# Holding back five weight transfers, and other readers, tiles and order for the last two groups of a mixture-of-experts kernel

## The chip, the cores and the metric

The kernel runs on one core of one Trainium2 chip. The metric is the device time of one execution in microseconds (us), taken as the median of several runs. The core has TensorE (PE in the profile, with its weight loads as PEld), VectorE (DVE), ScalarE (ACT), GpSimd (POOL) and SyncE (SP). SyncE only issues transfers here. GpSimd adds in SBUF and also issues the weight transfers, from the same queue of instructions.

## The reference

An attention with a feature map feeds a mixture of experts that is weighted with a balanced routing matrix P. Cut to what matters:

```python
proj = einsum('bhsd,df->bhsf', x, w_phi); proj -= max(abs(proj), -1)
phi  = concatenate([exp(proj), exp(-proj)], -1)          # for q and k
attn = (phi(q) @ (phi(k).T @ v)) / (phi(q) @ sum(phi(k)) + 1e-06)
x    = attn.transpose(0, 2, 1, 3).reshape(4608, 512)
P    = exp(x @ w_gate - max); 8 times: rows /= sum, columns /= sum, P *= N / E
out  = zeros((4608, 512))
for e in range(8):                       # w1[e]: 512 x 1024, w2[e]: 1024 x 512
    h = maximum(x @ w1[e], 0.0)
    out += P[:, e:e + 1] * (h @ w2[e])
```

There are 8 batches, 8 heads, 576 positions and a head width of 64, all float32 at the borders of the kernel.

## The kernel before

The attention, the routing and expert 0 come first. Experts 1 to 7 then run in one loop at the end of the kernel, and the change is in that loop. The 4608 tokens are nine groups: groups 0 to 7 have 512 tokens each and group 8 gathers the last 64 tokens of every batch. The sum over the experts stays in SBUF in float32, one tile `acc[g]` for each group (4 row tiles of 128 x 512). In the order listings `acc_4271` is group 6, `acc_4272` is group 7, `acc_4273` is group 8, and `acc_76` to `acc_80` with `acc_4270` are groups 0 to 5.

**Products.** Both matrix products of an expert are done with seven block products in place of eight, as Strassen and Winograd do. `up7` makes h = relu(x w1) for a pair of groups, `down7` makes h w2 for one group. The seven products of `down7` are called X1, X2, X3, X4, Y1, Z1 and Z2. X1 to X4 add up in one PSUM bank, Z1 and Z2 in another, and Y1 has a third; after each product the bank is read, because every partial sum belongs to some block of the output. Four of the products need sums of blocks of h, which VectorE makes ahead in four `S` tiles of two halves each, eight instructions (line L1013, `S<-hT`). For group 7 of the last expert these sums lie in tiles of the ring of h itself, so they read `hT<-hT`. The weights are summed in the same way (L1013, `T<-w` and `w<-w`, 1024 columns each).

**Who reads a bank.** `read` lets VectorE do acc = acc + P * bank in two instructions (L1305) where the product's name is in `by_dve`. Otherwise `read2` lets ScalarE copy the bank, scaled with P, into a tile `V` in two instructions (L1315), and GpSimd adds that tile to acc (L1319). In the usual group X2, Z2 and X4 go to VectorE and X1, Y1, Z1 and X3 go the other way. In groups 6 and 7 of the last expert the lists differ.

**Order of the work.** `ORDER` is a list written by hand that mixes the seven products of a group with the products of `up7` of groups that come later; group g's `down7` runs while later groups' h is made, so groups 6, 7 and 8 of expert e are finished while expert e + 1 has begun. The last expert takes group 8 first, and its groups 6 and 7 are left over: `END` interleaves their products by hand, "a" for group 6 and "b" for group 7. All operations are recorded with what they read and write and with a planned duration; a list scheduler, `Plan`, gives each engine its order, and the program is issued in that order. What an engine really waits for on the chip is set by the tiles that its instructions touch. A string in the lists of reads and writes, such as "sums of h", is a name that only the planner knows.

**Weights.** `load_w` (L378) asks GpSimd's queue for two transfers per expert, w1 and w2, of 2 MB in float32 each, cast to bfloat16 on the way, into two buffers each. An expert's weights are asked for about an expert ahead.

**Stores.** After the last expert SP sends acc to HBM. For groups 6 and 7 each block of two row tiles by 256 columns goes when its last product has been read (L982), and one block is cut into two transfers: `one`.

Of the kernel before, what the change touches and what calls it, by code (L numbers as in the profile page):

```python
# [228 lines left out]
def kernel(  # L229
# [16 lines left out]
    E = moe_w_gate.shape[1]  # L246
# [27 lines left out]
    acc = [accp.tile([128, 4, DD], FP32, name=f"acc{g}", tag=f"acc{g}") for g in range(NA)]  # L274
# [12 lines left out]
    late = {}  # L287
# [7 lines left out]
    def act(el, fn, r=(), w=()):  # L295
        plan.op("ACT", el / 1200.0 + 0.09, 0.22, fn, r, w)
# [4 lines left out]
    def pool(el, fn, r=(), w=()):  # L301
        plan.op("POOL", el * 1.64e-3 + 0.17, 0.25, fn, r, w, shared=True)

    def dma(queue, nbytes, rate, fn, r=(), w=()):

        plan.op(queue, 0.8 if queue == "POOL" else 0.6, 0.0, fn, r, w, (), nbytes / rate / (125 / 100))
# [52 lines left out]
    def new(tag):  # L359
        return banks.new(int(tag[1])) if tag in ("P1", "P2") else R[tag].new()  # L360

    def grant(tag, slot, ops):

        b = Buf(R[tag])
        b.slot = slot
        for o in ops:
            o.bufs.append(b)
            b.left += 1
# [6 lines left out]
    def load_w(e, r=()):  # L375
        w1, w2 = new("w1"), new("w2")
        for w, src in ((w1, moe_w1), (w2, moe_w2)):
            dma("POOL", 2 << 20, 280, lambda w=w, src=src: nc.gpsimd.dma_start(  # L378
                out=w(), in_=src[e].rearrange("(c p) f -> p c f", p=128)),
                r, [(w, i, j) for i in range(2) for j in range(2)])  # L380
        return w1, w2
# [365 lines left out]
    def xkeys(g, dc=None):  # L747
        if g < 8:
            return [("xT", g, i) for i in range(NP)] if dc is None else [("xT", g, dc)]
        return [("xTr", b, h) for b in range(B) for h in range(2)]  # L750
# [44 lines left out]
    def akey(g):  # L795
        return ["late"] * (g >= NA) + ["P"] * (g >= 9)
# [182 lines left out]
    def store(g, ts, js=(), nt=1):  # L979
        if len(js):  # L980
            cols = slice(256 * js[0], 256 * js[-1] + 256)
            dma("SP", len(js) * nt << 17, 320, lambda: nc.sync.dma_start(  # L982
                out=out[g * S:g * S + SM].rearrange("(p j) d -> p j d", j=NJ)[:, ts:ts + nt, cols],
                in_=acc[g][:, ts:ts + nt, cols]),
                [("acc", g, ts + n, j) for j in js for n in range(nt)],
                [("out", g, ts, j) for j in js])
        elif g < 8:
            if ts % 2:
                dma("SP", 1 << 19, 320, lambda: nc.sync.dma_start(
                    out=out[g * S:g * S + SM].rearrange("(p j) d -> p j d", j=NJ)  # L990
                    [:, ts - 1:ts + 1], in_=acc[g][:, ts - 1:ts + 1, :]),
                    [("acc", g, t, j) for t in (ts - 1, ts) for j in range(2)], [("out", g, ts)])
        else:
            for i in range(2):
                b = 2 * ts + i
                rows = slice(i * 64, i * 64 + 64)
                dma("SP", 1 << 17, 320, lambda b=b, rows=rows: nc.sync.dma_start(
                    out=out[b * S + SM:(b + 1) * S], in_=acc[8][rows, ts, :]),
                    [("acc", 8, ts, j) for j in range(2)], [("out", 8, b)])
# [79 lines left out]
    def pair_sums_x(p):  # L1079

        X = [new("S") for _ in range(4)]

        def x(n):
            return lambda: X[n]().rearrange("p (k a) b -> p k (a b)", k=2)

        b11, b12, b21, b22 = pq(p, 0, 1), pq(p, 0, 0), pq(p, 1, 1), pq(p, 1, 0)
        for n, y, z, r in ((0, b12, b11, ["sums of x"]), (1, b22, x(0), [X[0]]),
                           (2, b22, b12, []), (3, b21, x(1), [X[1]])):
            sub(dve, 1024, x(n), y, z, ALU.subtract,
                xkeys(2 * p) + xkeys(2 * p + 1) + ["late"] + r,  # L1090
                [X[n]] + (["sums of x"] if n == 1 else []))
            dma("SP", 1 << 18, 250, lambda n=n: nc.sync.dma_start(out=Xd[p][n], in_=x(n)()),
                [X[n]], [("Xd", p, n)])

    def sums_x(g):

        X = [new("S") for _ in range(2)]

        def x(n):
            return lambda: X[n // 2]()[:, n % 2 * 2:n % 2 * 2 + 2]  # L1100

        b11, b12, b21, b22 = xq(g, 0, 1), xq(g, 0, 0), xq(g, 1, 1), xq(g, 1, 0)
        for n, y, z, r in ((0, b12, b11, []), (1, b22, x(0), [0]), (2, b22, b12, []),
                           (3, b21, x(1), [1])):
            sub(dve, 512, x(n), y, z, ALU.subtract,
                xkeys(g) + ["late", "sums of x"] + [(X[i // 2], i % 2) for i in r]
                + ([(X[1], "slot")] if n == 2 else []),
                [(X[n // 2], n % 2)] + ([(X[1], "slot")] if n == 0 else []))
        for i in range(2):
            dma("SP", 1 << 18, 250, lambda i=i: nc.sync.dma_start(  # L1110
                out=Xd[4][i], in_=X[i]().rearrange("p (k a) b -> p k (a b)", k=2)),
                [(X[i], n) for n in range(2)], [("Xd", 4, i)])
# [129 lines left out]
    def down7(e, g, H, B7, last=False):  # L1242
# [13 lines left out]
        late = akey(g)  # L1256
# [36 lines left out]
                    r + r2 + (["P"] if e else late) + list(more), first)  # L1293

        by_dve = ("X2", "Z2", "X4")
        if e == E - 1 and g in (6, 7):
            by_dve = (("X2", "X3", "X4", "Z1", "Z2") if g == 6 else ("X3", "X4", "Z1", "Z2"))

        def read(bank, i, j, name):

# [9 lines left out]

        def read2(bank, i, j):

            u = new("V")
            for n in range(2):
                act(390, lambda n=n: nc.scalar.activation(  # L1315
                    out=u()[:, n, :], in_=bank()[:, 256 * n:256 * n + 256], func=ACT.Copy,
                    bias=0.0, scale=P[:, 4 * g + 2 * i + n, e:e + 1]), [bank, "P"],
                    [(u, n), "order of V"])
            pool(670, lambda: nc.gpsimd.tensor_tensor(  # L1319
                out=acc[g][:, 2 * i:2 * i + 2, 256 * j:256 * j + 256],  # L1320
                in0=acc[g][:, 2 * i:2 * i + 2, 256 * j:256 * j + 256], in1=u(), op=ALU.add),
                [(u, 0), (u, 1)], [("acc", g, 2 * i + n, j) for n in range(2)])

        if e == 1 and g < 9:
            for ts in range(4):
# [35 lines left out]
        def stores(names):  # L1361
            if e < E - 1:
                return
            if g not in (6, 7):
                for ts in range(4 if len(names) == len(all_) else 0):
                    store(g, ts)
                return
            for i, j, by in ((0, 0, {"X1", "Y1"}), (0, 1, {"X2", "Z2"}), (1, 1, {"Z1", "X3"}),
                             (1, 0, {"X4"})):
                if by <= names and (i, j) not in stored:  # L1370
                    stored.add((i, j))
                    one = g == 7 and (i, j) == (0, 1)
                    for n in range(2 if one else 1):
                        store(g, 2 * i + n, (j,), 1 if one else 2)

# [10 lines left out]

    ORDER = "X1 x10 w10 x11 X2 x20 y10 x21 Z1 y11 X3 w11 x30 x31 x40 x41 w20 Y1 w21 X4 Z2".split()
    END = (
        "aX1 aX2 aY1 aZ1 aZ2 bX1 aX3 bX2 bZ1 bY1 bX3 aX4 bX4 bZ2").split()
    queue = []  # L1390

    def pop():
        if not queue:
            return None
        e, g, H, B7 = queue.pop(0)
        return down7(e, g, H, B7, (e, g) == (E - 1, 7))

    for e in range(1, E):
        w1, w2 = load_w(e, ["late"])
        if e == 1:  # L1400
            for p in range(4):
                pair_sums_x(p)
            sums_x(8)
            for p in range(4):
                seen = {}
                for key in xkeys(2 * p):
                    for d in plan.readers.get(key, []):
                        seen[id(d)] = d
                grant("X", p, seen.values())
        A7, B7 = sums_w(e, w1, w2)  # L1410
        for p in (range(5) if e < E - 1 else (4, 0, 1, 2, 3)):
            X = load_x(p)
            gs = (2 * p, 2 * p + 1) if p < 4 else (8,)
            H = [[[new("hT") for _ in range(2)] for _ in range(2)] for _ in gs]
            un = up7(A7, p, X, H, ["up0"])
            for half in range(len(gs)):
                dn = pop()
                for n in ORDER:
                    if len(n) == 3:
                        un[n[:2], int(n[2]) + 2 * half]()  # L1420
                    elif dn is not None:
                        dn(n)
            queue += [(e, g, h, B7) for g, h in zip(gs, H)]
# [34 lines left out]
```

## Time and profile before

| | before |
|---|---|
| runs | 1037.2, 1037.89, 1035.61 us |
| median | 1037.2 us |
| the profiled execution: its own time / its span | 1037.74 us / 1036.0 us |
| granted TensorE clock, mean over the span | 0.997 |
| TensorE busy | 1008.2 us, 97% of the span |
| VectorE / ScalarE / GpSimd busy | 877.0 / 706.7 / 467.4 us |
| weight transfers of `load_w` and expert 0 | 14 of 1024 KB as written, median 9.2 us to landing |
| stores of acc | 12 of 512 KB and 9 smaller ones at the end |

The profile is of one execution. "Busy" counts instructions that ran, and a busy TensorE can still run at half its clock. In the rows a line is start, duration, engine, line of the code, operation, output and inputs with their shapes, and a count; square brackets give the idle time of the engine before it and who ended that. Line numbers are those of the kernel before. A row of the chain of waits says which work, or which wait, led to the end of the run.

### The profile page before, as it was taken

To read this page: it belongs to the slowest core of one execution; us is meant where nothing else is said; L and a number is where in the kernel's file an instruction comes from. 1 tells how busy PE (TensorE), PEld (TensorE's weight loads), DVE (VectorE), ACT (ScalarE), POOL (GpSimd) and SP (SyncE) were. 2 spreads that over 40 slices of the span, in tenths; PEclk is the share of its full clock that TensorE was granted. 3 is DMA by queue.
4 is the path that set the end of the run, shared out by engine and by line. 5 is a ranking of instruction groups with operands and counts; after the bars stand their busy time and mean duration, and the time that the engine had idled before them with its cause. 6 is when DMAs were issued, how large, how long until landed. Compare 5 with 4: busy or idle time off the path is not lost.

```text
span 1036.0 us, 21792 instructions
## 1 busy us (share of the span) xinstructions
PE 1008.2 (97%) x7856; PEld 692.1 (67%) x7974; DVE 877.0 (85%) x1875; ACT 706.7 (68%) x1571; POOL 467.4 (45%) x535
## 2 busy tenths in 40 slices
PE   7899999999999999999999999999999999999997
PEld 5666666644566766676667666776667666776665
DVE  7999998987787888888888888888888788887887
ACT  7999999845688766666666665666666665656662
POOL 5776775400244444444444444444444444344443
PEclk9999999999999999999999999999999999999998
DMA  9998995095311441132311341134113411204323
GB/s 254 182 170 134 187 161 103 2 229 144 75 44 50 92 82 42 42 89 60 78 41 57 77 92 43 41 62 83 46 47 92 82 42 42 62 22 123 133 92 122
DMA packets 124700, 93.77 MB, mean 91 GB/s; under 512 B 47456, under 2 KB 116640, under 8 KB 124592
## 3 DMA queue, kind: packets, MB, share of 16 engines
q1 hardware_dynamic: 90832, 68.44, 24.2%
q0 software_dynamic: 33680, 23.90, 16.5%
q8 instruction: 62, 1.02, 0.4%
q14 instruction: 46, 0.38, 0.1%
q10 hardware_dynamic: 80, 0.03, 0.0%
HBM read 94.98 MB, written 14.16 MB: 105 GB/s over the span
## 4 chain that ended last, share of the span: by engine, by line
PE 84%; DVE 5%; issue 1%; ACT 1%; DVEq 0%; ACTq 0%
PE P L1130 39%; PE P L1164 31%; PE P L484 13%; DVE acc L1305 1%; DVE hT L1194 1%; PE P L683 1%; DVE w L1013 1%; DVE hT L1013 1%; PE P L722 0%; DVE S L1013 0%; ACT q L480 0%; DVE m L476 0%; PE P L688 0%; ACT U L1190 0%; ACT hT L776 0%
## 5 line engine op out<-in xcount | busy, mean ns | idle before, releaser
L1319 POOL TENSOR_TENSOR acc<-acc,V 128x512 f32<-128x512 f32 x249 | 320.8, 1301 | 432.9 <-ACT V L1315 429.5
L1190 ACT COPY U<-P 128x512 f32<-128x512 f32 x378 | 215.8, 588 | 145.7 <-PE P L1164 81.6
L1315 ACT ACTIVATE V<-P 128x256 f32<-128x256 f32 x498 | 217.8, 476 | 127.0 <-PE P L1130 123.4
L1194 DVE CUSTOM_DVE_ANT_0 hT<-P,U 128x512 bf16<-128x512 f32 x378 | 252.6, 687 | 44.0 <-ACT U L1190 22.7
L1130 PEld LDWEIGHTS <-S 128*128 128x128 bf16 x1984 | 194.8, 98 | 55.7 <-issue 3.2
L1305 DVE SCALAR_TENSOR_TENSOR acc<-P,acc 128x256 f32<-128x256 f32 x384 | 164.3, 477 | 65.1 <-PE P L1130 62.9
L1164 PE MATMUL P<-xT,w 128*128 128x512 bf16 x674 | 191.3, 379 | 3.6 <-DVE acc L1305 2.3
L1130 PEld LDWEIGHTS <-hT 128*128 128x128 bf16 x1544 | 151.1, 98 | 57.7 <-DVE hT L1194 0.7
L1164 PE MATMUL P<-xT,T 128*128 128x512 bf16 x550 | 158.1, 379 | 1.8
L1130 PE MATMUL P<-w,hT 128*128 128x256 bf16 x1016 | 145.3, 273 | 0.4 <-DVE hT L1194 0.3
L1130 PE MATMUL P<-T,S 128*128 128x256 bf16 x1056 | 137.8, 274 | 3.1 <-DVE acc L1305 2.7
L1164 PEld LDWEIGHTS <-w 128*128 128x128 bf16 x896 | 87.6, 98 | 62.0 <-issue 0.7
L1130 PE MATMUL P<-w,S 128*128 128x256 bf16 x928 | 123.9, 274 | 0.6
L1013 DVE TENSOR_TENSOR S<-hT 128x512 bf16<-128x512 bf16 x248 | 103.1, 433 | 19.2 <-PE P L1130 18.4
L1164 PEld LDWEIGHTS <-T 128*128 128x128 bf16 x672 | 65.7, 98 | 58.9 <-issue 4.2
L476 DVE TENSOR_REDUCE m<-P 128x4 f32<-128x512 f32 x128 | 83.6, 678 | 4.0 <-PE P L484 3.1
L609 POOL TENSOR_TENSOR v<-v_m,em 128x512 bf16<-128x512 f32 x64 | 67.0, 1047 | 42.8 <-ACT em L480 38.7
L1199 ACT ACTIVATE hT<-P 128x512 bf16<-128x512 f32 x126 | 74.5, 598 | 9.9 <-PE P L1164 9.6
L484 PE MATMUL P<-xT,w 128*128 128x512 bf16 x271 | 71.7, 379 | 0.9 <-ACT q L480 0.3
L484 PE MATMUL P<-w,hT 128*128 128x512 bf16 x272 | 69.7, 379 | 0.8 <-DVE m L476 0.2
L1130 PE MATMUL P<-T,hT 128*128 128x256 bf16 x528 | 70.4, 273 | 0.1
L480 ACT ACTIVATE q<-P 128x512 bf16<-128x512 f32 x128 | 69.4, 637 | 1.2 <-PE P L484 0.9
(107 smaller groups left out, 1168.8 us busy)
## 6 DMA issues: line engine op xcount, KB each, us to landing
xT<-xd SPq DMA_DIRECT2D x168, 128.0 KB, 2.2
w<-in_moe_w_dram POOLq DMA_DIRECT2D x14, 1024.0 KB, 9.2
v_m<-in_v_dram SPq DMA_DIRECT2D x14, 512.0 KB, 4.7
out_dram<-acc SPq DMA_DIRECT2D x12, 512.0 KB, 3.1
X<-xd SPq DMA_DIRECT2D x42, 128.0 KB, 2.2
early<-xd SPq DMA_DIRECT2D x42, 128.0 KB, 2.1
xd<-S SPq DMA_DIRECT2D x18, 256.0 KB, 2.9
qk<-in_k_dram POOLq DMA_DIRECT2D x12, 256.0 KB, 5.8
```

The costliest lines, as they stand in the source:

```text
L476: dve(el, lambda: nc.vector.tensor_reduce(out=dst(), in_=src(), axis=AX.X, op=ALU.max, apply_absolute_value=True), r, w)
L480: act(el, lambda: nc.scalar.activation(out=dst(), in_=src(), func=ACT.Exp, bias=0.0, scale=scale), r, w)
L484: nc.tensor.matmul(out_, lhsT=lhsT, rhs=rhs, start=start, stop=stop)
L1013: lambda: f.tensor_tensor(out=out_(), in0=x(), in1=y(), op=op), r, w, **kw)
L1130: pe(256, lambda i=i, k=k, z=z: nc.tensor.matmul(bank()[:, 256 * i:256 * i + 256], lhsT=lhs(k, i), rhs=rhs(k), start=first and z, stop=k = ...
L1164: pe(512, lambda k=k: nc.tensor.matmul(bank[fp](), lhsT=f()[:, k, 128 * fp:128 * fp + 128], rhs=rhs(k), start=first and k == 0, stop=k == ...
L1190: act(512, lambda: nc.scalar.copy(out=u[fp][n]().rearrange("p a b -> p (a b)"), in_=x[fp]()), [x[fp]], [u[fp][n]])
L1194: dve(500, lambda: nc.vector._custom_dve(ADD_SAT, out=out_(fp, i, j), in0=halves_(bank[fp]()), in1=flat(u[fp][n]()), s0=3.0e38, s1=0.0), [ ...
L1199: act(512, lambda: nc.scalar.activation(out=out_(fp, i, j), in_=halves_(x[fp]()), func=ACT.Relu, bias=0.0, scale=1.0), [x[fp]], [okey(fp, ...
L1305: dve(330, lambda n=n, ts=ts: nc.vector.scalar_tensor_tensor(out=acc[g][:, ts, 256 * j:256 * j + 256], in0=bank()[:, 256 * n:256 * n + 256 ...
L1315: act(390, lambda n=n: nc.scalar.activation(out=u()[:, n, :], in_=bank()[:, 256 * n:256 * n + 256], func=ACT.Copy, bias=0.0, scale=P[:, 4 ...
L1319: pool(670, lambda: nc.gpsimd.tensor_tensor(out=acc[g][:, 2 * i:2 * i + 2, 256 * j:256 * j + 256], in0=acc[g][:, 2 * i:2 * i + 2, 256 * j: ...
```

## The change

Four edits. First, the weight transfers of experts 3 to 7 (those asked for while an expert above 1 is on) get a read of group 8's acc as an extra dependence, for w1 and w2. Second, the readers of banks in the last expert's groups 6 and 7 change: VectorE takes X2, X3, X4, Y1, Z1, Z2 of group 6 (before X2, X3, X4, Z1, Z2) and X2, X4, Z2 of group 7 (before X3, X4, Z1, Z2). GpSimd makes five additions in both, aX1, aY1, bX1, bX2, bY1 before and aX1, bY1, bX1, bZ1, bX3 now. Third, in these two groups ScalarE copies into `U`, a ring of four tiles, and the planner holds the additions for "sums of h". Fourth, the hand-written `END` is another one, and the block of the last stores that is cut in two is (1, 0) of group 6, whose last product is X4.

```diff
-        if e == E - 1 and g in (6, 7):
-            by_dve = (("X2", "X3", "X4", "Z1", "Z2") if g == 6 else ("X3", "X4", "Z1", "Z2"))
+        ending = e == E - 1 and g in (6, 7)
+        if ending:
+            by_dve = by_dve + ("X3", "Y1", "Z1") if g == 6 else by_dve
...
-            u = new("V")
+            u = new("U" if ending else "V")
...
-                [(u, 0), (u, 1)], [("acc", g, 2 * i + n, j) for n in range(2)])
+                [(u, 0), (u, 1)] + ["sums of h"] * ending,
+                [("acc", g, 2 * i + n, j) for n in range(2)])
...
-                    one = g == 7 and (i, j) == (0, 1)
+                    one = (g, i, j) == (6, 1, 0)
...
-        "aX1 aX2 aY1 aZ1 aZ2 bX1 aX3 bX2 bZ1 bY1 bX3 aX4 bX4 bZ2").split()
+        "aX1 bY1 aX2 bX1 bX2 bZ1 aZ1 aX3 aY1 aZ2 bX3 bX4 bZ2 aX4").split()
...
-        w1, w2 = load_w(e, ["late"])
+        w1, w2 = load_w(e, ["late"] + [("acc", 8, ts, j) for ts in range(4) for j in range(2)
+                                       if e > 1])
```

How this moves instructions is seen in two places. The first is GpSimd's queue at a weight transfer in the middle of the loop, from group 6 to the w2 transfer; the names behind `DMA` are the weight tiles, and `waits` lists the engines and transfers whose semaphores the instruction waits for. Before:

```order
L1319 TENSOR_TENSOR acc_4271<-acc_4271,V 128x2x256 [waits Activation_49] x2
L378 DMA w_8603<-in_moe_w_dram 128x4x1024 [waits DMASW6_49,DVE_49,PE_49]
L1319 TENSOR_TENSOR acc_4271<-acc_4271,V 128x2x256 [waits Activation_49,Pool_49]
L1319 TENSOR_TENSOR acc_4271<-acc_4271,V 128x2x256 [waits Activation_49]
L1319 TENSOR_TENSOR acc_4272<-acc_4272,V 128x2x256 [waits Activation_49] x2
L1319 TENSOR_TENSOR acc_4272<-acc_4272,V 128x2x256 [waits Activation_49,Pool_49]
L1319 TENSOR_TENSOR acc_4272<-acc_4272,V 128x2x256 [waits Activation_49]
L1319 TENSOR_TENSOR acc_4273<-acc_4273,V 128x2x256 [waits Activation_49] x2
L1319 TENSOR_TENSOR acc_4273<-acc_4273,V 128x2x256 [waits Activation_49,Pool_49]
L1319 TENSOR_TENSOR acc_4273<-acc_4273,V 128x2x256 [waits Activation_49]
L378 DMA w_8946<-in_moe_w_dram 128x8x512 [waits DMASW7_49,DVE_49,PE_49]
```

And now:

```order
L1320 TENSOR_TENSOR acc_4271<-acc_4271,V 128x2x256 [waits Activation_49] x2
L1320 TENSOR_TENSOR acc_4271<-acc_4271,V 128x2x256 [waits Activation_49,Pool_49]
L1320 TENSOR_TENSOR acc_4271<-acc_4271,V 128x2x256 [waits Activation_49]
L1320 TENSOR_TENSOR acc_4272<-acc_4272,V 128x2x256 [waits Activation_49] x2
L1320 TENSOR_TENSOR acc_4272<-acc_4272,V 128x2x256 [waits Activation_49,Pool_49]
L1320 TENSOR_TENSOR acc_4272<-acc_4272,V 128x2x256 [waits Activation_49]
L1320 TENSOR_TENSOR acc_4273<-acc_4273,V 128x2x256 [waits Activation_49] x2
L1320 TENSOR_TENSOR acc_4273<-acc_4273,V 128x2x256 [waits Activation_49,Pool_49]
L1320 TENSOR_TENSOR acc_4273<-acc_4273,V 128x2x256 [waits Activation_49]
L378 DMA w_8947<-in_moe_w_dram 128x4x1024 [waits DMASW6_49,DVE_49,PE_49]
L378 DMA w_8960<-in_moe_w_dram 128x8x512 [waits DMASW7_49,DVE_49,PE_49]
```

The w1 transfer has moved from the middle of group 6's four additions to behind group 8's last one, directly ahead of the w2 transfer, which stays where it was. On VectorE the sums of that tile move with it (`T<-w_8603` was the first of them, `w_8603<-w_8603` the second). Before, on VectorE, from group 8's last reads to the first reads of group 0 (`acc_76`):

```order
L1305 SCALAR_TENSOR_TENSOR acc_4273<-P,acc_4273 128x256 x4
L1013 TENSOR_TENSOR S<-hT 128x512
L1013 TENSOR_TENSOR S<-hT,S 128x512
L1013 TENSOR_TENSOR S<-S,hT 128x512
L1013 TENSOR_TENSOR T<-w_8603 128x1024
L1013 TENSOR_TENSOR S<-hT,S 128x512
L1194 ISA hT<-P,U 128x512 x2
L1013 TENSOR_TENSOR S<-hT 128x512
L1305 SCALAR_TENSOR_TENSOR acc_76<-P,acc_76 128x256 x2
```

And now, from group 0's last reads to the second sum:

```order
L1306 SCALAR_TENSOR_TENSOR acc_76<-P,acc_76 128x256 x4
L1013 TENSOR_TENSOR S<-hT,S 128x512
L1013 TENSOR_TENSOR T<-w_8947 128x1024
L1013 TENSOR_TENSOR S<-hT 128x512
L1306 SCALAR_TENSOR_TENSOR acc_77<-P,acc_77 128x256 x2
L1194 ISA hT<-P,U 128x512
L1013 TENSOR_TENSOR S<-hT 128x512
L1013 TENSOR_TENSOR w_8947<-w_8947 128x2x512
```

The first sum of w1 has moved from behind group 8's last reads to behind group 0's. The sum in place, which stood ahead of group 1's first reads (`acc_77`), follows them.

The second place is GpSimd's queue in the last two groups of the last expert. Before:

```order
L1319 TENSOR_TENSOR acc_4271<-acc_4271,V 128x2x256 [waits Activation_49]
L1319 TENSOR_TENSOR acc_4271<-acc_4271,V 128x2x256 [waits Activation_49,Pool_49]
L1319 TENSOR_TENSOR acc_4272<-acc_4272,V 128x2x256 [waits Activation_49]
L1319 TENSOR_TENSOR acc_4272<-acc_4272,V 128x2x256 [waits DVE_49,Activation_49]
L1319 TENSOR_TENSOR acc_4272<-acc_4272,V 128x2x256 [waits Activation_49,Pool_49]
```

And now:

```order
L1320 TENSOR_TENSOR acc_4271<-acc_4271,U 128x2x256 [waits Activation_49]
L1320 TENSOR_TENSOR acc_4272<-acc_4272,U 128x2x256 [waits Activation_49]
L1320 TENSOR_TENSOR acc_4272<-acc_4272,U 128x2x256 [waits Activation_49,Pool_49]
L1320 TENSOR_TENSOR acc_4272<-acc_4272,U 128x2x256 [waits Activation_49]
L1320 TENSOR_TENSOR acc_4272<-acc_4272,U 128x2x256 [waits Activation_49,Pool_49]
```

The second addition went to group 6's block of the first one and waited for it; now it goes to group 7's and waits for ScalarE alone. No addition waits for VectorE any more, and the sums of h stand on VectorE where they stood, eight in a row behind group 6's.

## The prediction

> **What bounds the kernel now.** I read the page first, then who TensorE waited for from 300 us on (the loop over the experts), then the chain of waits and the timeline of the last 25 us. The page's lines on the engines, the granted clock and the chain:
>
> ```profile
> span 1036.0 us, 21792 instructions
> ...
> PE 1008.2 (97%) x7856; PEld 692.1 (67%) x7974; DVE 877.0 (85%) x1875; ACT 706.7 (68%) x1571; POOL 467.4 (45%) x535
> PEclk9999999999999999999999999999999999999998
> PE 84%; DVE 5%; issue 1%; ACT 1%; DVEq 0%; ACTq 0%
> ```
>
> TensorE bounds it: 97% busy at full clock in all but the last slice. The change removes no product, so it can only win where TensorE stands still or is slow. The waits of TensorE between 300 and 1010 us, and the chain of waits at the end:
>
> ```profile
> PE P L1164 <- DVE acc L1305: 2.3, 4, 0.6
> ...
> 1016.18 5.90 DVE hT L1013 x8
> 1022.08 0.80 DVE acc L1305 x2
> 1022.88 0.04 issue
> 1022.92 6.48 PE P L1130 x42
> ```
>
> So there are two targets: four waits of 0.6 us at the borders of experts, and one stretch at the end where VectorE's eight sums for group 7 hold TensorE. The windows of the end show both prices of that stretch (window, length, busy PE, PEld, DVE, ACT, POOL, then granted clock):
>
> ```profile
> 1019.60:1023.03 3.43, 0.69 (x8) 0.47 (x6) 3.43 (x5) 0.84 (x2) 2.05 (x2) 1.00 0.21 76
> 1023.03:1026.44 3.41, 3.41 (x18) 2.35 (x17) 1.50 (x4) 0.00 (x0) 0.00 (x0) 0.50 0.00 0
> 1026.44:1029.80 3.36, 3.36 (x32) 2.95 (x31) 2.93 (x7) 1.57 (x4) 1.42 (x2) 1.00 0.44 156
> ```
>
> TensorE is nearly idle in the first, and in the second it runs at clock 0.50, which costs 3.41 x 0.50 = 1.7 us.
>
> **The w1 transfers.** One of the four waits, in the timeline of GpSimd, VectorE and TensorE, with a free sum of the same form as the last row:
>
> ```profile
> 570.41 0.79 POOL L378 DMA_DIRECT2D w<-in_moe_w_dram  x1 [2.19 <-PE P L1130]
> 571.23 2.50 POOL L1319 TENSOR_TENSOR acc<-acc,V 128x512 f32<-128x512 f32 x2
> 572.05 2.23 DVE L1013 TENSOR_TENSOR w<-w 128x1024 bf16<-128x1024 bf16 x1
> 574.93 0.38 PE L1164 MATMUL P<-xT,w 128*128 128x512 bf16 x1
> 575.90 0.38 PE L1164 MATMUL P<-xT,w 128*128 128x512 bf16 x1 [0.59 <-DVE acc L1305]
> 573.85 0.81 PE L1164 MATMUL P<-xT,w 128*128 128x512 bf16 x3
> 350.63 0.68 DVE L1013 TENSOR_TENSOR w<-w 128x1024 bf16<-128x1024 bf16 x1
> ```
>
> The transfer holds GpSimd's queue to 571.2, its two additions then run back to back to 573.73, and the weight sum, issued at 572.05 in the middle of the first, ends only at 574.28: 2.23 us where 0.68 is free. A sum of two SBUF tiles doesn't get in between two additions that follow each other without a gap. The reads behind it come late, and TensorE starts its next matmul 0.97 us after the last; three in 0.81 us are (0.81 - 0.38) / 2 = 0.22 apart, so 0.75 us is lost. What stands there without a transfer is seen at the last expert, for which no weights are asked any more:
>
> ```profile
> 901.89 2.50 POOL L1319 TENSOR_TENSOR acc<-acc,V 128x512 f32<-128x512 f32 x2 [2.58 <-ACT V L1315]
> 903.14 1.79 DVE L1013 TENSOR_TENSOR T<-w 128x1024 bf16<-128x1024 bf16 x1
> 906.04 0.89 PE L1130 MATMUL P<-xT,w 128*128 128x256 bf16 x4
> 905.60 0.60 PE L1130 MATMUL P<-X,T 128*128 128x256 bf16 x4
> ```
>
> The additions start 1.25 us ahead of the sum instead of 0.82, the sum takes 1.79, and four matmuls take 0.89 where four take 0.60: 0.29 lost. So the move gives 0.75 - 0.29 = 0.46 at each of four borders, -1.8 us. Bounds: nothing, if the additions wait for ScalarE anyway, and 4 x 0.75 = -3.0, if the sum escapes both additions.
>
> At its new place the transfer stands behind group 8's last addition. Who waits for it there:
>
> ```profile
> 598.54 0.92 POOL L378 DMA_DIRECT2D w<-in_moe_w_dram  x1
> 602.92 2.71 POOL L1319 TENSOR_TENSOR acc<-acc,V 128x512 f32<-128x512 f32 x2 [3.46 <-ACT V L1315]
> ...
> 613.61 0.68 DVE L1013 TENSOR_TENSOR w<-w 128x1024 bf16<-128x1024 bf16 x1
> DMA to landing us min/median/max: 8.1/9.2/17.9
> ```
>
> GpSimd is idle for 3.46 us behind the w2 transfer of today, so a second one of 0.8 to 0.9 us holds up no addition: nothing, and 0.9 if that idle time were not there. Landing: w1 issued at 598.5 is there at 607.7 by the median, and its first sum now follows group 0's last reads, which is the stretch ahead of 613.61, about 612; w2 behind it lands at 616.4 at the latest (598.54 + 17.9, the longest of all loads). With the longest landing for w1 itself the sum would wait 4 us; I take nothing, since w1 is first in its queue. The sums' own collisions with additions at the new place are a rival below.
>
> **The end: additions against sums.** The additions and copies in the stretch, from the timeline; the row of sum 8 is VectorE's:
>
> ```profile
> 1016.73 1.57 ACT L1315 ACTIVATE V<-P 128x256 f32<-128x256 f32 x4 [3.96 <-PE P L1130]
> 1017.64 2.74 POOL L1319 TENSOR_TENSOR acc<-acc,V 128x512 f32<-128x512 f32 x2 [3.53 <-ACT V L1315]
> 1019.62 0.84 ACT L1315 ACTIVATE V<-P 128x256 f32<-128x256 f32 x2 [1.32 <-PE P L1130]
> 1020.54 1.26 POOL L1319 TENSOR_TENSOR acc<-acc,V 128x512 f32<-128x512 f32 x1
> 1020.59 1.49 DVE L1013 TENSOR_TENSOR hT<-hT 128x512 bf16<-128x512 bf16 x1
> L1013 DVE TENSOR_TENSOR hT<-hT x8: 415/418/1489, 1016.1 to 1020.6; 128x512 bf16<-128x512 bf16 x8
> ```
>
> Free sums take 0.42 us and follow each other at 0.34. Three of the eight took about 1.49, each behind one addition: 2.74 us for two additions of 1.26 leaves a gap, because the second goes to the block of the first and waits for it, and a sum got in there.
>
> By its name the change holds the additions until all sums are made. The program doesn't: the compiled additions wait for ScalarE and for their own kind only, since "sums of h" is no tile, and ScalarE's copies into U depend on no sum. So the additions go as soon as their copies are there. aX1 and bY1 write different blocks, and nothing keeps a gap between them: about 17.64 to 20.16 (all of 1000 us more here). Sum 6 waits for both and hands over a pitch later, at 20.50; sum 7 gets in narrowly ahead of bX1, whose copies are done at 1019.62 + 0.84 = 20.46 (today's addition behind them starts at 20.54). Then bX1 and bZ1 run pressed together (bZ1's bank is read next by ScalarE, 0.84 us for the pair, and U has four tiles where V had two): 20.46 + 2 x 1.26 = 22.98, and sum 8 ends 0.42 later at 23.4 instead of 22.08. That is +1.3 us on the path: aX2's reads (0.80) and X3 of group 6 behind them at about 24.25.
>
> Bounds: if the sums keep getting in one by one, 0; if one more pair holds them, +2.5, an addition for each.
>
> **Behind the stretch.** The rest of the end in TensorE's timeline, and SP's last transfers:
>
> ```profile
> 1022.92 1.79 PE L1130 MATMUL P<-T,S 128*128 128x256 bf16 x8 [2.74 <-DVE acc L1305]
> 1029.22 1.04 PE L1130 MATMUL P<-w,hT 128*128 128x256 bf16 x8
> 1030.35 1.03 PE L1130 MATMUL P<-T,hT 128*128 128x256 bf16 x8
> 1030.33 2.48 SPq L982 DMA_DIRECT2D out_dram<-acc  x5
> ```
>
> TensorE is idle for 2.74 us now and for 4.0 then, so I keep the stretch at half clock: no difference. Two matmuls fewer are left behind the stretch (56 for 58, 0.11 each: -0.2). Eight matmuls take 1.04 us, so those of 1030.35 could have followed at 1029.22 + 8 x 0.11 = 1030.09 and waited 0.26 for reads of their bank; in the new order the last two products have banks of their own: -0.26. The last products of both groups now come together and leave SP one issue more behind the last read, at 2.48 / 5 = 0.5 each: +0.4. The five additions stay five, and the last (bX3) has three products behind it, so it is not late. Together: +1.3 - 0.2 - 0.3 + 0.4 = +1.2 us.
>
> **Sum.** -1.8 + 1.2 = -0.6 on the profiled execution's 1037.74 (span 1036.0 and 1.74 around it) is 1037.1. That execution lies 0.54 above the median of the three runs, so against 1037.2 I say **1036.6 us**. A change within 0.2%, or 2.07 us (1035.1 to 1039.3), can't be told from none, as the runs alone spread over 2.3.
>
> **Rivals.**
>
> *Sums get in between.* By the trace a sum got in wherever GpSimd paused, even for 0.08 us; if the new additions are issued with such pauses, the end costs -0.1 instead of +1.2, and the time is 1037.2 - 1.9 = **1035.3**. For it: three of three sums did so here. Against: both additions at 571.23, pressed together, held one sum. The Trainium skill, "SBUF — State Buffer", on port contention, says that an instruction of VectorE with two SBUF inputs and one of GpSimd hold the shared ports for the whole instruction and whichever starts first blocks the other; by it alone a waiting sum would be blocked by one addition, and this rival's time would follow. The trace differs: 2.23 us at 572.05 spans two.
>
> *The wait is real.* If the additions did stand behind the sums, all eight would end by 16.09 + 8 x 0.34 = 1018.9, TensorE would not stand (-2.74) and keep its clock (-1.7): -4.4 at the end, and with -1.8 **1031.0**. Against it: no such wait in the compiled rows.
>
> *The clock holds.* If the longer idle time falls otherwise against the clock's windows, -1.7: **1034.9**. For it: one case in the trace alone, 0.69 us busy in a window of 3.43 and then 0.50. The Trainium skill, "TensorE: Matmul & The Clock Gate", Part 1, has the clock halved after an idle window of about 3.4 us. The trace agrees in length, though TensorE was not idle in all of it; an idle time of 4.0 us then makes it no less likely.
>
> *Slower: the moved sums collide.* The in-place sum of w1 at 613.61 is free today. One group later or behind other reads, it may meet a pair of additions, as that of 572.05 did: 0.75 for each of five experts is +3.75, so 1036.6 + 3.75 = **1040.4**. It decides from 0.55 at each. Against it: behind group 1's first reads, it starts after the pair that runs with them.
>
> **Chances.** Forecast 0.40 (own range 1035.0 to 1038.5), sums between 0.19, a real wait 0.14, clock 0.11, collision 0.16. Range 1033.9 to 1040.4: it leaves out the real wait and about 0.05 beyond. Faster: 0.14 + 0.10 + 0.07 + 0.04 of the forecast = 0.35. Slower: 0.13 of the collision + 0.04 of the forecast = 0.17. The rest, 0.48, is within 0.2%.
>
> **What would show it.** Right: a weight sum of 1.8 us and no wait of 0.6 for TensorE at the borders; in the end two pairs of additions without a gap, two long sums, of which one is over 2.5 us, TensorE idle for about 4 us, one window at 0.50. Wrong: eight sums at 0.42 us and additions behind them (the wait is real), all sums under 1.5 (they get in), or `w<-w` of 2 us at new places with waits of L1164 behind them (collision).

## The result and the profile after

The changed kernel takes 1035.3 us (median of 22 runs, 1032.48 to 1038.17), the kernel before 1037.25 (22 runs): ratio 0.998 with a 95% interval of 0.9971 to 0.9988. That is 1.95 us faster, just inside the 0.2% that the prediction had set as its bound for no change; with 22 runs of each the interval leaves out 1, so a small gain is real. The profiled execution took 1034.76 us.

The page's lines on the span and the engines, and who TensorE waited for between 300 and 1005 us (waiting engine, releaser, us in total, times, longest):

```profile
span 1032.9 us, 21788 instructions
PE 1007.7 (98%) x7856; PEld 692.4 (67%) x7974; DVE 874.4 (85%) x1875; ACT 707.5 (68%) x1571; POOL 466.8 (45%) x535
PE P L1164 <- DVE acc L1306: 0.6, 4, 0.2
```

The four waits at the borders are still there, but 0.2 us long in place of 0.6. One of them in the timeline, with the weight sum and the two additions beside it:

```profile
569.56 2.50 POOL L1320 TENSOR_TENSOR acc<-acc,V 128x512 f32<-128x512 f32 x2 [2.58 <-ACT V L1316]
570.81 1.79 DVE L1013 TENSOR_TENSOR w<-w 128x1024 bf16<-128x1024 bf16 x1
573.69 0.38 PE L1164 MATMUL P<-xT,w 128*128 128x512 bf16 x1
574.23 0.38 PE L1164 MATMUL P<-xT,w 128*128 128x512 bf16 x1 [0.16 <-DVE acc L1306]
349.81 0.69 DVE L1013 TENSOR_TENSOR w<-w 128x1024 bf16<-128x1024 bf16 x1
```

The additions start 1.25 us ahead of the sum in place of 0.82, so the first is all but over when the sum is issued; the sum waits for the second alone and takes 1.79, as at the last expert before. TensorE starts 0.54 us after its last matmul, so 0.32 is lost where 0.75 was. The last row stands ahead of the first moved instruction: the kernel before had this sum at 350.63, so 0.8 us of the 3.1 between the two spans is the spread of executions and not the change.

The end, in the chain of waits, VectorE's line L1013, and the timelines of GpSimd and ScalarE:

```profile
1013.25 5.89 DVE hT L1013 x8
1019.14 0.80 DVE acc L1306 x2
1019.98 6.21 PE P L1130 x40
L1013 DVE TENSOR_TENSOR hT<-hT x8: 418/420/1492, 1013.2 to 1017.7; 128x512 bf16<-128x512 bf16 x8
1013.74 1.57 ACT L1316 ACTIVATE U<-P 128x256 f32<-128x256 f32 x4 [3.90 <-PE P L1130]
1014.65 5.61 POOL L1320 TENSOR_TENSOR acc<-acc,U 128x512 f32<-128x512 f32 x4 [3.47 <-ACT U L1316]
PE P L1130 <- DVE acc L1306: 2.6, 1, 2.6
```

The eight sums take 5.89 us on the chain where they took 5.90, and TensorE waits 2.6 us where it waited 2.7. From the first sum to the end of the span it is 1032.9 - 1013.2 = 19.7 us, and 1036.0 - 1016.1 = 19.9 before. The changed end is worth 0.2 us in these two traces.

### The profile page after: what moved, and what is told of

It is laid out like the page before. It is cut to its first block, busy times and chain, and to the rows that moved or that the text cites. A ratio compares the mean times of both kernels' runs of the same rounds, so it can differ in the third digit from the quotient of the medians.

```text
span 1032.9 us, 21788 instructions
## 1 busy us (share of the span) xinstructions
PE 1007.7 (98%) x7856; PEld 692.4 (67%) x7974; DVE 874.4 (85%) x1875; ACT 707.5 (68%) x1571; POOL 466.8 (45%) x535
## 4 chain that ended last, share of the span: by engine, by line
PE 90%; DVE 6%; DMA 1%; issue 1%; ACT 1%; SPq 0%; POOL 0%; DVEq 0%; ACTq 0%
PE P L1130 40%; PE P L1164 30%; PE P L484 17%; DVE acc L1306 1%; PE P L683 1%; DMA acc<-in_q_dram 1%; DVE hT L1194 1%; DVE m L476 1%; DVE w L1013 1%; PE P L722 1%; DVE hT L1013 1%; DVE S L1013 0%; SPq L406 0%; PE P L688 0%; DVE xb L703 0%
## 5 line engine op out<-in xcount | busy, mean ns | idle before, releaser
L1320 POOL TENSOR_TENSOR acc<-acc,V 128x512 f32<-128x512 f32 x244 | 313.9, 1298 | 433.4 <-ACT V L1316 430.0
L1316 ACT ACTIVATE V<-P 128x256 f32<-128x256 f32 x488 | 212.8, 477 | 122.1 <-PE P L1130 118.6
L1013 DVE TENSOR_TENSOR S<-hT 128x512 bf16<-128x512 bf16 x248 | 105.1, 439 | 19.3 <-PE P L1130 18.3
L480 ACT ACTIVATE k<-P 128x512 bf16<-128x512 f32 x128 | 68.8, 633 | 2.2 <-PE P L484 1.3
```

What stands on the lines that cost most here:

```text
L480: act(el, lambda: nc.scalar.activation(out=dst(), in_=src(), func=ACT.Exp, bias=0.0, scale=scale), r, w)
L1013: lambda: f.tensor_tensor(out=out_(), in0=x(), in1=y(), op=op), r, w, **kw)
L1316: act(390, lambda n=n: nc.scalar.activation(out=u()[:, n, :], in_=bank()[:, 256 * n:256 * n + 256], func=ACT.Copy, bias=0.0, scale=P[:, 4 ...
L1320: pool(670, lambda: nc.gpsimd.tensor_tensor(out=acc[g][:, 2 * i:2 * i + 2, 256 * j:256 * j + 256], in0=acc[g][:, 2 * i:2 * i + 2, 256 * j: ...
```

## The experiments

**Each part alone.** The first kernel is the one before with only this edit; the second is the changed one with only this edit taken back.

```diff
-        w1, w2 = load_w(e, ["late"])
+        w1, w2 = load_w(e, ["late"] + [("acc", 8, ts, j) for ts in range(4) for j in range(2)
+                                       if e > 1])
```

> The kernel before with the moved w1 transfers alone; the last two groups as they were. Theory (the move of the transfers carries the whole gain, the end none): TensorE's waits at the four borders fall from 0.6 to 0.2 us, the end stays as before with sums at about 1.49, and the time is 2.0 us under the kernel before, ratio 0.998. The forecast's sum (-1.8 at the borders, +1.2 at the end) would give the same 1.8 to 2.0 here, and this kernel would then be 1.2 us faster than the whole change. Rival (the end carries the gain): no change here, ratio 1.000.

> The changed kernel with the w1 transfers back at their old place: the changed end alone. Theory (sums get in one by one in the new order too): the four waits of 0.6 are back, the end has three sums of about 1.49 and one wait of TensorE of 2.6, and the time is that of before, within 0.3 us, ratio 1.000. By the forecast's sum it would be 1.2 us slower, ratio 1.001. Rival (the end carries the gain): 2 us faster, ratio 0.998.

The transfers alone: 1034.9 us against 1037.21, ratio 0.9975 (0.9965 to 0.9986). The end alone: 1036.44, ratio 0.9997 (0.9985 to 1.0008). Who TensorE waited for from 300 us to the end, first with the transfers moved alone, then with the end changed alone:

```profile
PE P L1130 <- DVE acc L1305: 2.7, 1, 2.7
PE P L1164 <- DVE acc L1305: 0.6, 4, 0.2
```

```profile
PE P L1130 <- DVE acc L1306: 2.6, 1, 2.6
PE P L1164 <- DVE acc L1306: 2.4, 4, 0.6
```

The parts are separate: the borders belong to the transfers, and the changed end gives nothing that can be told from none. The theory held, the forecast's +1.2 and the rival that the end carries the gain fell.

**A wait that is real.** The changed kernel, with the wait that its edit names put into the program by a tile that the instruction really reads:

```diff
+            if ending and last_sum:
+                sl, key = last_sum.pop()      # the last sum's tile, from group 7's down7
+                pool(1, lambda: nc.gpsimd.tensor_copy(out=held[:, 0:1], in_=sl()[:, 3, 255:256]), [key], ["held"])
...
-                [(u, 0), (u, 1)] + ["sums of h"] * ending,
+                [(u, 0), (u, 1)] + ["sums of h", "held"] * ending,
```

> The changed kernel with one small copy on GpSimd (128 x 1, out of the last sum's tile into a tile of its own) ahead of the first addition of the last two groups, so that the additions do wait for all eight sums; nothing else moves. Theory (the additions hold the sums): all eight sums take 0.42 us, TensorE's wait of 2.6 us at the end goes, the clock does not halve (another 1.6), and the time falls by 4.2 us against the changed kernel, to about 1031, ratio to before 0.994. Rival (the late additions hold the banks, U or the stores in place of the sums): a new wait of TensorE behind ScalarE or later last stores, gain under 1 us. Rival on the clock (it halves for another reason than the idle stretch): the window at 0.50 stays, gain 2.6 us alone.

It took 1031.93 us, ratio to before 0.9946 (0.9934 to 0.9958), and on another chip 1031.3, ratio 0.9955 (0.9942 to 0.9967).

> The kernel with the real wait once more, for comparison on the same chip: 1031 to 1032 us, ratio to before 0.9945.

The sums and GpSimd in this kernel's timeline, and two windows of 3.4 us behind the sums (busy us of PE, PEld, DVE, ACT, POOL, then the granted clock):

```profile
L1013 DVE TENSOR_TENSOR hT<-hT x8: 418/418/419, 1013.8 to 1016.1; 128x512 bf16<-128x512 bf16 x8
1016.62 0.19 POOL L1322 COPY held<-hT 128x1 bf16<-128x1 bf16 x1 [4.81 <-DVE hT L1013]
1016.76 4.95 POOL L1323 TENSOR_TENSOR acc<-acc,U 128x512 f32<-128x512 f32 x4
1016.40:1019.80 3.40, 3.40 (x33) 3.05 (x32) 2.73 (x8) 1.68 (x4) 3.18 (x4) 1.00 0.01 5
1019.80:1023.20 3.40, 3.40 (x33) 3.05 (x32) 3.00 (x8) 0.84 (x2) 2.17 (x3) 1.00 0.52 173
```

No sum is long any more, the additions run behind them, TensorE is busy throughout, and the clock stays at 1.00. From the first sum to the end it is 1029.4 - 1013.8 = 15.6 us in place of 19.7: 4.1 less, where the theory said 4.2; by the ratios to the kernel before it is 3.5 (0.998 and 0.9946). VectorE reads PSUM banks beside the late additions, and those reads are not held: they take 0.47 to 0.49 us each.

**Which part of the rest is needed for that.** Once the real wait with the old tiles V, once with the old order, readers and tiles (the transfers stay moved in both).

> The kernel with the real wait, but ScalarE's copies of the last two groups go into V (two tiles) as before, in place of U (four). Theory (four tiles are needed once the additions wait): the third and fourth copy wait for the first two additions, about 0.8 us, and some of that reaches TensorE through the banks: 0.3 to 1 us over the kernel with the real wait. Rival (the tiles don't matter): the same time, no wait of TensorE in the last 20 us.

> The kernel with the moved transfers alone (old end, old readers, V) and the small copy ahead of its first addition of the last two groups, so that the old end's additions wait for the sums. Theory (holding the sums was all that was wrong at the end, whatever the order): sums at 0.42 us, no window at half clock, about 4 us under the kernel with the moved transfers alone, near 1031. Rival (the new order, readers and tiles are needed to live with late additions): copies wait for V, TensorE waits 0.5 us or more behind ScalarE or the banks, and 1 us or more of the gain is lost.

With V it took 1031.35 us, ratio 0.9948 (0.9933 to 0.9963); with the whole old end 1031.27, ratio 0.9945 (0.9928 to 0.9961). TensorE's waits in the last 30 us, with V and then with the old end:

```profile
PE P L1130 <- ACT V L1316: 1.0, 1, 1.0
L1013 DVE TENSOR_TENSOR hT<-hT x8: 418/418/420, 1013.2 to 1015.6; 128x512 bf16<-128x512 bf16 x8
```

```profile
PE P L1130 <- DVE acc L1305: 0.4, 1, 0.4
L1013 DVE TENSOR_TENSOR hT<-hT x8: 418/418/420, 1014.7 to 1017.0; 128x512 bf16<-128x512 bf16 x8
```

With the new order and V, a wait of 1.0 for ScalarE appears (the copies wait for a tile), and from the first sum to the end of the span of 1029.2 it is 16.0 us: 0.4 more than with U, as that theory said, but by one trace each: the runs' times don't show it (1031.35 with V; 1031.93 and 1031.3 with U). With the old order it is 1030.2 - 1014.7 = 15.5. So neither U nor the new order is needed: holding the additions is the whole gain that the runs can tell, and the old end lives with it as well. The theory held there, and the rival's loss of 1 us did not come.

**Why some sums wait for two additions.** In the kernel before, the weight sum at 572.05 spanned two additions; in the changed end every long sum waited for one, although two of the three pairs of neighbouring additions had no gap between them. The first idea was the sum's width.

```diff
-        sub(eng, 1024, t1, q(w2, *b12), q(w2, *b11), ALU.subtract, ...
+        eng(1024 * 0.6, lambda: [nc.vector.tensor_tensor(
+            out=t1()[:, h:h + 2], in0=q(w2, *b12)()[:, h:h + 2], in1=q(w2, *b11)()[:, h:h + 2], op=ALU.subtract)
+            for h in (0, 2)], ...
```

> The kernel before, with one weight sum of each expert (the one in place that stood in the middle of the two additions at the borders, 1024 columns) written as two instructions of 512 columns, nothing else moved. Theory by width (a sum of 512 columns gets in where one additon follows the other, one of 1024 doesn't): the first half, issued 0.8 us into the first addition, takes about 0.7 us, the second addition gets longer by 0.2, and the second half waits for that. Theory by timing (a sum issued so late in an addition misses the gap whatever its width): the first half takes about 1.9 us and spans both additions.

The first half sum and the two additions (one execution, 1038.28 us):

```profile
571.50 2.50 POOL L1320 TENSOR_TENSOR acc<-acc,V 128x512 f32<-128x512 f32 x2
572.32 1.97 DVE L1055 TENSOR_TENSOR w<-w 128x512 bf16<-128x512 bf16 x1
```

The half sum spans both as well: width is not it. The next idea came from the traces. At a border of the kernel before, ScalarE's copies for the second addition are done when the sum is issued at 572.05:

```profile
571.07 0.84 ACT L1315 ACTIVATE V<-P 128x256 f32<-128x256 f32 x2
```

They end at 571.91. At the changed end the four copies that start at 1013.74 end at 1015.31, when sum 6, whose predecessor had started at 1014.50, was already waiting. So the turn would go to whoever asks first. The test makes the fourth addition of a border ask late:

```diff
+            gap = 1 < e < E - 1 and g == 6 and name == "Y1"
+            pool(670, lambda: (gap and nc.gpsimd.tensor_copy(out=held[:, 1:2], in_=acc[g][:, 2, 256:257]), nc.gpsimd.tensor_tensor(...
```

> The kernel with the real wait, and at the five borders of experts 2 to 6 a small GpSimd copy (128 x 1, out of the block that group 6's third addition has just written) between the third and the fourth addition, so that the fourth is asked for only after the third has ended. Theory (the shared port is given in the order of asking: a sum waits for the second of two additions where that one's copies were ready ahead of the sum, and for one alone where they came after it): the weight sum, which is issued as the third addition ends, gets in ahead of the fourth and takes 0.7 to 0.9 us instead of 1.79, TensorE's 0.32 us at the five borders goes, and the time falls by 1.2 to 1.6 us under the real wait. Rival (GpSimd's queue goes first, whatever the order of asking): the sum takes 1.8 to 2.1 us and the time stays or rises by 0.5.

```profile
570.34 1.26 POOL L1324 TENSOR_TENSOR acc<-acc,V 128x512 f32<-128x512 f32 x1 [2.58 <-ACT V L1316]
571.67 0.65 POOL L1324 CAST held<-acc 128x1 bf16<-128x1 f32 x1
572.28 1.26 POOL L1324 TENSOR_TENSOR acc<-acc,V 128x512 f32<-128x512 f32 x1
571.59 0.68 DVE L1013 TENSOR_TENSOR w<-w 128x1024 bf16<-128x1024 bf16 x1
```

The sum gets in, the one-column copy takes 0.65 us where the one at the end took 0.19, and the trace has no wait of TensorE for another engine from 300 us to the end. It took 1029.83 us against 1036.48, ratio 0.9937 (0.9923 to 0.9951), 1.5 us under the real wait on the same chip. This is the fastest version found, with both kernels beaten by more than their spread.

**What the old transfer did.** The other question at the borders is whether the transfer cost its time in GpSimd's queue or in itself. The first attempt put a copy of 0.47 us in its place, and missed: it ran in an idle stretch, the additions stood 1.24 us ahead of the sum as without it, and the waits stayed at 0.2 us (one execution, 1035.23 us), which says nothing.

> The changed kernel with a copy of 128 x 256 in place in the tile V on GpSimd ahead of group 6's third addition, where the w1 transfer was issued before, in experts 2 to 6; no result changes. Theory (the old transfer cost its time in GpSimd's queue, by which the two additions started 0.4 to 0.5 us later and both hit the weight sum): TensorE's waits at the borders are 0.5 to 0.7 us again, with no transfer there. Rival (the transfer itself, its descriptors or its writes, slowed the sum): the waits stay at 0.2.

```profile
569.08 0.47 POOL L1321 COPY V<-V 128x256 f32<-128x256 f32 x1 [1.63 <-ACT V L1316]
570.03 2.50 POOL L1321 TENSOR_TENSOR acc<-acc,V 128x512 f32<-128x512 f32 x2 [0.47 <-ACT V L1316]
571.27 1.79 DVE L1013 TENSOR_TENSOR w<-w 128x1024 bf16<-128x1024 bf16 x1
```

The second copy was held by ScalarE's last write and so did move the additions; the third writes a tile of its own; the fourth is the second in the kernel before, with the transfer in place.

```diff
+            held_up = 1 < e < E - 1 and g == 6 and name == "X3"
+            pool(670, lambda: (held_up and nc.gpsimd.tensor_copy(out=u()[:, 1, :], in_=u()[:, 1, :]), nc.gpsimd.tensor_tensor(...
```

> As the copy at the borders before, which had found an idle stretch and moved no addition, but of the half of V that ScalarE writes last, so that it must hold the two additions by about 0.45 us. Theory (the queue): the weight sum takes 2.2 us, its additions start 0.8 us ahead of it, and the four waits of TensorE are 0.5 to 0.7 us with no transfer there. Rival (the transfer itself): the waits stay at 0.2.

> As the second copy at the borders, but the GpSimd instruction ahead of the third addition writes a small tile of its own (128 x 200), so that the addition follows it without waiting for it. Open is why the sum got in behind one addition in the second copy's kernel, and spanned two in the kernel before, where additions, copies and sum stood in the same places to 0.05 us. Theory A (it was the transfer: behind one issued, the two additions go through together): the sum again takes about 1.0 us and TensorE loses nothing at the borders. Theory B (it was the addition's wait for an instruction of its own engine, which opens the queue): without it the sum spans both additions, 2.2 us, and TensorE's waits are 0.5 to 0.7.

> The kernel before, transfers at their old place, with the second copy (in place, of the half of V that ScalarE writes last) between the transfer and the two additions at the borders, so that both theories stand against each other with the transfer there. Theory A: the sum spans both additions, and as they start 0.4 us later it takes 2.6 us and TensorE loses about 1.2 at each border. Theory B: the sum gets in behind the first addition, about 1.4 us, and TensorE loses under 0.3.

The additions and the sum at one border, for the second copy, the third and the fourth:

```profile
570.67 2.95 POOL L1321 TENSOR_TENSOR acc<-acc,V 128x512 f32<-128x512 f32 x2
571.46 1.03 DVE L1013 TENSOR_TENSOR w<-w 128x1024 bf16<-128x1024 bf16 x1
570.47 0.84 ACT L1316 ACTIVATE V<-P 128x256 f32<-128x256 f32 x2
```

```profile
570.53 2.94 POOL L1321 TENSOR_TENSOR acc<-acc,V 128x512 f32<-128x512 f32 x2
571.54 0.80 DVE L1013 TENSOR_TENSOR w<-w 128x1024 bf16<-128x1024 bf16 x1
```

```profile
570.31 2.94 POOL L1320 TENSOR_TENSOR acc<-acc,V 128x512 f32<-128x512 f32 x2
570.66 1.46 DVE L1013 TENSOR_TENSOR w<-w 128x1024 bf16<-128x1024 bf16 x1
1019.00:1022.40 3.40, 3.39 (x32) 3.02 (x32) 2.77 (x7) 0.51 (x2) 0.00 (x0) 1.00 0.14 50
```

In all three the sum got in behind one addition and the second addition grew from 1.27 to about 1.7; none of the three traces has a wait of TensorE for another engine at the borders. This refutes more than it settles. The second copy's kernel has additions 0.79 us ahead of the sum and the second addition's copies done 0.15 us ahead of it, as the kernel before had 0.82 and 0.14, and it came out the other way: so the order of asking, read from the copies, is not the whole rule. The third fells the theory of the addition's wait for its own engine, and the fourth the theory of the transfer, at least with a copy between it and the additions. What the three share, and the kernel before lacks, is a GpSimd instruction on SBUF directly ahead of the pair. Open is why that matters, and whether a transfer directly ahead of a pair presses it together; this was not tried further. The other traces can't part the two. Sums that span two additions stand only where the transfer is directly ahead of the pair: all 12 at the four borders of the kernel before, of the changed end alone and of the halved sums. And in no pair with neither a transfer nor a copy ahead did a sum meet the first addition when the second's copies were long done: they came after the sum, or 0.07 us ahead of it at most, or the first addition was over. One execution each, so times are not compared: 1034.16, 1034.28 and 1032.17 us.

## Why the prediction was right or wrong

**Borders: the size right, the reason not shown.** -1.8 was said, and 4 x (0.75 - 0.32) = 1.7 came, with the sum at 1.79 as the last expert's row had it. Not foreseen were three places in the middle of experts (623, 734 and 844 us before). There, in the old order of VectorE, a sum `S<-hT` met an addition (1.42 us at 621.55) and the reads behind it came late. Five matmuls, before and after:

```profile
622.80 1.38 PE L1164 MATMUL P<-xT,w 128*128 128x512 bf16 x5
```

```profile
621.13 1.24 PE L1164 MATMUL P<-xT,w 128*128 128x512 bf16 x5
```

That is 0.14 each, 0.4 together. The reason given, that the transfer pushed the additions later in GpSimd's queue, is not shown: copies that push them as far (additions 0.79 us ahead of the sum, where the transfer had 0.82) let the sum in.

**The end: wrong by 1.4 us.** The step that failed is the rule that a sum "doesn't get in between two additions that follow each other without a gap": by it sum 6 was to wait for aX1 and bY1 together, and sum 8 for bX1 and bZ1. That nothing keeps a gap between them was right. The rows of that place now, GpSimd's and VectorE's:

```profile
1014.65 1.39 POOL L1320 TENSOR_TENSOR acc<-acc,U 128x512 f32<-128x512 f32 x1 [3.47 <-ACT U L1316]
1016.00 1.45 POOL L1320 TENSOR_TENSOR acc<-acc,U 128x512 f32<-128x512 f32 x1
1014.50 1.83 DVE L1013 TENSOR_TENSOR hT<-hT 128x512 bf16<-128x512 bf16 x2
```

No gap, and yet the sum ended at 1016.33, 0.33 into the second addition, which took 1.45 in place of 1.26. One row of two pressed additions (572.05) had been made a rule. The trace before already held the counterexample, and the prediction did not look for it:

```profile
877.91 2.68 POOL L1319 TENSOR_TENSOR acc<-acc,V 128x512 f32<-128x512 f32 x2 [2.85 <-ACT V L1315]
878.75 0.71 DVE L1013 TENSOR_TENSOR S<-hT,S 128x512 bf16<-128x512 bf16 x1
```

The second of these two additions begins as the first ends; their 2.68 us are longer than 2.50 because it took 1.45 behind the sum.

Behind the stretch the sum was -0.2 - 0.3 + 0.4 = -0.1, and -0.2 came: from TensorE's restart to the end it is 1032.9 - 1020.0 = 12.9 us and was 1036.0 - 1022.9 = 13.1. So the +1.3 of the stretch is the term that was wrong, and 0.0 came. With the end at +1.2 it was 1036.6; with -0.2 it is the rival in which sums get in between (chance 0.19), 1035.3 by its working and 1035.3 by measurement. That agreement is in part luck: the rival had sums get in where GpSimd pauses, and two of three got in without a pause, and it knew nothing of the 0.4 in the middle of experts. The terms of the traces together make -1.7 - 0.4 - 0.2 = -2.3, the medians -1.95. The Trainium skill's rule there ("SBUF — State Buffer", on port contention, whichever starts first holds the shared ports for the whole instruction) agrees in that the end's sums of about 1.49 and those of the three copies' kernels waited for one addition; the sums of the four borders before, at 2.21 to 2.23, exceed it. Nor was it the whole instruction here: sums that were issued 1.12 to 1.14 us into an addition of 1.27 were not held (0.43 us).

**The wait that is not in the program: right**, and its price too. The reading of the compiled waits said that "sums of h" holds nothing, and the rows of the end agree. The rival with a real wait was worked out as -4.4 at the end (its 16.09 + 8 x 0.34 is 1018.8, not 1018.9, which changes nothing), and the kernel that has one shows 1029.4 - 1013.8 = 15.6 where the kernel before has 19.9, -4.3.

**The moved sums' collision** did not come. The in-place sum of w1 at its new place, and the landing of the two transfers that are now issued together at one border:

```profile
614.15 0.69 DVE L1013 TENSOR_TENSOR w<-w 128x1024 bf16<-128x1024 bf16 x1
DMA to landing us min/median/max: 8.2/10.8/13.3
```

The sum is free, and w1, the first in its queue, lands ahead of it.

**The clock: right, but not by the length of the wait alone.** 4.0 us of idle time were said and 2.6 came, and the clock halved as before. The changed kernel's row (its window of 3.40 us begins 0.27 ahead of the half clock, so it shows 0.54):

```profile
1020.10:1023.50 3.40, 3.40 (x19) 2.48 (x18) 2.07 (x6) 0.00 (x0) 0.16 (x1) 0.54 0.30 102
```

But in the fourth copy's kernel TensorE waited 2.7 us in the same place, and the window behind it, the last row of its fence, stands at 1.00. So 1.7 us hang on where the idle stretch falls, not on its length alone. The clock records of the fourteen traces show where: the granted clock changes only at steps of 3.41 us, which lie elsewhere in each execution. In the kernel before, the idle time from 1020.18 to 1022.92 lies within one step; in the fourth copy's kernel a step ends at 1018.26 and parts it into 1.98 and 0.75 us. In these traces, from the clock's first rise on, every step with 2.03 us or more without a matmul is followed by half clock, every one with 1.87 or less by full clock; of three at 1.97 to 1.98, two are followed by half. A bound near 2.0 us of idle time in one step fits all of this, but no run was made to test it.

## What to carry to other kernels

In a kernel planned like this one, a wait exists only where an instruction touches a tile that another one writes; a name in the planner's list makes no wait on the chip, so look for the wait in the compiled rows before pricing it, and if the wanted wait is not there, a one-column read can make it. Here, additions on GpSimd that are not urgent belong behind VectorE's sums of two SBUF tiles, or need an opening ahead of the second of a pair. Before one row is made a rule, look through the same trace for every other place where the same two instructions meet.

## What the runs showed of the hardware

How long an addition of GpSimd holds a sum on VectorE depends on when the sum is issued. From 300 us on in the kernel before, 38 sums that take 0.42 us free (128x512) were issued while an addition ran (1.27 us free). Twelve, issued 1.12 to 1.14 us after its start, took 0.43 or less, and one more, issued as the addition started, got ahead of it. The other 25 took longer the earlier they came: up to 1.54 at the addition's start, 1.20 at 0.35, 0.71 at 0.84. So a hold ended about 1.13 us after the addition's start, and none of the 38 waited for two. Two additions were spanned only by the weight sums at the four borders, with the transfer directly ahead of the pair, at 2.21 to 2.23 for 0.68; one short GpSimd instruction ahead of the pair brought that to between 0.80 and 1.46. And after the same idle time of TensorE, 2.74 us, the clock was 0.50 for a window in the kernel before and stayed at 1.00 behind it in another, where the stretch fell across two of the clock's steps.
